# Exponent factors picked out by TensorE, the output gradient's copy moved, and more buffers, in a one-core layer kernel

## The chip, the cores and the metric

The kernel runs on one core of a Trainium2 chip. The metric is the device time of one execution in microseconds (us), of which three runs are shown. The core has TensorE (PE, with its weight loads PEld), VectorE (DVE), ScalarE (ACT), GpSimd (POOL) and SyncE (SP, which here only issues transfers). ACT and POOL issue transfers too.

## The reference

A layer with a state-space convolution and a gated feed-forward block, computed forward (`out_0`) and backward (`out_1` to `out_12`, the gradients of its inputs). L = 2048 tokens, D = 576 channels, N = 128 states per channel, F = 4608 hidden units. Cut to what matters:

```
xn = layernorm(A_u)
dt = exp(log_dt);  logdA = dt * (A_re + 1j * A_im)
K  = einsum("dn,dnl,dn->dl", C, exp(logdA * l), dt * B).real      # 576 x 2048 kernel of the convolution
s  = irfft(rfft(K) * rfft(xn)) + xn * Dskip                       # causal convolution over l
g  = silu((silu(xn @ w1) * (xn @ w3)) @ w2)
out_0 = A_u + s * g;  and the gradients for grad_out
```

`exp(logdA * l)` has a real factor exp(dt * A_re * l), which this text calls the **exponent factor**, and a sine and cosine part. With l = 64a + b each is split in a part over a (32 values) and a part over b (64 values), so per channel 96 values per state are computed.

## The kernel before, in words

**Prologue.** The tokens are loaded as 16 tiles of 128; those with an odd number are first turned back to front by a copy in DRAM (`odd_A_u`, and `odd_grad_out` for the output gradient), which later loads read. DVE makes the layer norm: statistics and scaling of the even tiles, then of the odd ones. PE turns the normalised tiles (`ln_turn`, ten sets of transposes through the PSUM pool `t_ps`, which has two buffers) and DVE copies each set to `xnT`.

**Exponent factors.** DVE multiplies dt and A_re (`rho`) and splits the product in three bf16 pieces (`pc`, in `split3`). To become the left operand of a matmul, the pieces must stand with 16 channels on the partitions: `split3` stores them in `PCS_dram[2]`, and three loads bring them back into `lhs_r` in that order. Then `early_exps` makes 54 tiles: PE multiplies `lhs_r` with the selector `sel_val` into a PSUM tile of 1024 columns (`e_ps`, two buffers), ACT takes the exponential into `E_k` (six buffers), SP stores it in `E_dram`. Many of these matmuls are issued twice, and 44 matmuls (line 370) with no use of their result run ahead of them. A Chain keeps the instructions of one engine in the order of the code; matmuls are placed behind a named lead.

**Spectra and selectors.** DVE folds the tiles (`xt<-xn_bf`), computes the angles (`thp` to `pc`, stored to `PCS_dram[0:2]`), and PE transforms the folded tokens (`early_spectrum`, line 635): 20 PSUM tiles go through `t_ps` and DVE, 12 through `e_ps` and ACT, as casts to `u_e`, stored to `UH_dram` from SP. Between them DVE builds `SEL` and the weights `Wr`, `Wi`.

**Main part.** `ffn_hidden` multiplies the tokens with w1 and w3 (lines 1121 and 1129, `pgu`), 72 steps; ACT makes `s_t` and `gu_t`, DVE `h_t`. `ssm_kernel` is woven into it: 36 chunks, each needing `lhs_t` (six small loads from `PCS_dram`), `E_l` (from `E_dram`) and matmuls into `et_ps` (line 712). Then the convolution (`ssm_conv`: `dft`, `take`, `inverse`), the feed-forward output, and the backward pass, most of the time. What stands on an engine's list is fixed by a scheduler from priorities (`pre` for the prologue, `at` later).

The copy of the odd tiles of grad_out (line 1012) is written in the convolution's `take`, but issued by GpSimd at 8.57 us.

Of the kernel before, what the change touches and what calls it, by code (L numbers as in the profile page):

```python
# [100 lines left out]
class K:  # L101
# [212 lines left out]
    def prologue(self, matp, selp, xp, gate):  # L314
# [8 lines left out]
        self.xnT = xp.tile([P, DT, L], BF16, name="xnT")  # L323
        self.PCS_dram = self.dram.tile([3, 3, D, N], BF16, name="PCS_dram")
        self.odd = {n: self.dram.tile([LT // 2, P, D], BF16, name="odd_" + n) for n in ("A_u", "grad_out", "out_0", "out_1")}
        mul = lambda e, o, a, b: e.tensor_tensor(out=o[:], in0=a[:], in1=b, op=ALU.mult)
        with pool(name="par_tmp", bufs=1) as tmp, pool(name="par_pc", bufs=2) as pcp, pool(name="sel_tmp", bufs=1) as st, \
                pool(name="ln_sb", bufs=1) as lsb, pool(name="ln_small", bufs=4) as small, pool(name="dftgen", bufs=1) as dg, \
                pool(name="ex_l", bufs=1) as lp, pool(name="ex_e", bufs=6) as ep, pool(name="ex_u", bufs=2) as up, \
                pool(name="ex_ps", bufs=2, space=PS) as eps, pool(name="t_ps", bufs=2, space=PS, side="right") as tps:  # L330
# [33 lines left out]
            self.dma_engines, self._dma_i = [self.sy, self.S], 0  # L364
            pc = self.split3(tmp, rho, 2)
            for k in range(3):
                self.sy.dma_start(out=LR_[k * 16:(k + 1) * 16], in_=self.PCS_dram[2, k].rearrange("(k p) n -> p k n", p=16))
            pw = eps.tile([P, 1024], FP32, name="e_ps")
            for k in range(44):
                nc.tensor.matmul(pw[:, 0:512], lhsT=pc[:, 2, 0, :], rhs=pc[:, 0, 0:4, :], start=True, stop=True)  # L370
            self.ln_load_odd(self.sy)
            self.pre(2)
            self.dft_phases()
            self.build_reader(SELR)
            self.pre(8)
            self.dft_sines()
# [4 lines left out]
            last = self.ln_stats(even[1:], small, last)  # L381
            self.ln_root(even, small, last)
            self.dma_engines, self._dma_i = [self.sy], 0
            turns = {14: 0, 15: 1, 20: 2, 21: 3, 22: 4, 23: 5, 24: 6, 25: 7, 26: 8, 27: 9}
            self.early_exps(SELR, LR_, ep, eps, 0, 18, turns)
            self.exps_last = self.S.prev
            next(gate)
            self.pre(18)
            self.ln_scale(even)
            self.pre(24)  # L390
            last = self.ln_stats(odd, small)
            self.ln_root(odd, small, last)
            self.ln_scale(odd)
            leads = sorted(turns)
            self.ln_turn(even, tps, leads[0:5])
            self.ln_turn(odd, tps, leads[5:10])
            self.dft_signs()
            self.dft_rows()
            self.pre(34)
            self.ln_fold()  # L400
            self.pre(38)
            thp = tmp.tile([P, DT, N], FP32, name="thp", tag="t1")
# [47 lines left out]

    def split3(self, tmp, src, q):
# [10 lines left out]
        for (c, p0, n, h, d1) in self.dsplit():  # L462
            self.dma(self.PCS_dram[q].rearrange("k (d h) n -> h d k n", h=2)[h, d1:d1 + n], pc[p0:p0 + n, :, c, :])
        return pc
# [133 lines left out]
    def early_exps(self, SELR, LR_, ep, ps, p0, p1, turns):  # L598
# [8 lines left out]
        for c2 in range(2 * p0, 2 * p1, 2):  # L607
            for o in range(0, 2 * TW, 1024):
                E = ep.tile([P, 1024], BF16, name="E_k")
                self.pre(17.5 + 1.07 * len(self.e_stores))  # L610
                pe = ps.tile([P, 1024], FP32, name="e_ps")
                n = len(self.exps)
                for k in (0, 1) if n in turns or n >= 40 else (0, 0, 1, 1):
                    ch, o1 = divmod(o + 512 * k, TW)
                    self.e_last = nc.tensor.matmul(pe[:, 512 * k:512 * k + 512], lhsT=LR_[:, c2 + ch, :],
                                                   rhs=SELR[:, o1:o1 + 512], start=True, stop=True)
                self.exps.append(self.e_last)
                self.S.activation(out=E[:], in_=pe[:], func=ACT.Exp)
                self.e_stores.append(nc.sync.dma_start(out=self.E_dram[c2 // 2, :, o:o + 1024], in_=E[:]))

    def early_spectrum(self, h, m, up, ps, name, copy, leads):
# [6 lines left out]
        for k0 in range(0, KT, 2):  # L628
            u = up.tile([P, 2, 2, 2, HW], BF16, name="u_e", tag="u" + name)
            for kt in range(k0, k0 + 2):  # L630
# [10 lines left out]
            for q in range(2):  # L641
                nc.sync.dma_start(out=self.UH_dram[2 * h + q, m, :, :, k0:k0 + 2], in_=u[:, q])

    def ssm_kernel(self, T0, TK, ps, ps1):
# [8 lines left out]
        with self.pool(name="kg_l", bufs=2) as lp, \  # L653
# [15 lines left out]
            def load_lhs(c0):  # L669
                t_ = lp.tile([P, GE, N], BF16, name="lhs_t")  # L670
                nc.gpsimd.memset(t_[:], 1.0)
                for k in range(3):
                    for q, r0 in enumerate((0, 64)):
                        nc.sync.dma_start(out=t_[r0 + k * DC:r0 + (k + 1) * DC],
                                          in_=self.PCS_dram[q, k, c0 * DC:(c0 + GE) * DC, :].rearrange("(k p) n -> p k n", p=DC))
                return t_
# [280 lines left out]
    def conv_half(self, h, T0, kp, up, rp, ypool, tp, spool, epool, ps):  # L957
# [27 lines left out]
        def take(b):  # L985
# [23 lines left out]
            self.cmul_acc(V[0], k2, kz, U[NB - 1 - b], tp, b == 0, False)  # L1009
            if h == 0 and b == NB - 1:  # L1010
                with self.tc.issue_after(self.tails[-1].ins):
                    nc.gpsimd.dma_start(out=self.odd["grad_out"][:], in_=self.turned(self.aps["grad_out"].flatten_outer_dims()))

        def inverse(m):
# [5 lines left out]
            for i in range(2):  # L1020
                even = self.idft_side(ps.tile([P, 512], FP32, name="et_ps"), V[0], 0, i, 1)
                odd = self.idft_side(ps.tile([P, 512], FP32, name="et_ps"), V[0], 1, i, 1)
                ev = epool.tile([P, W], FP32, name="ev")
                nc.scalar.copy(out=ev[:], in_=even)
                s_t = spool.tile([P, 2, W], BF16, name="s_t")
# [1060 lines left out]
def kernel(  # L2086
# [35 lines left out]
    with k.ctx:  # L2122
# [8 lines left out]
        with k.pool(name="xT", bufs=1) as xp, k.pool(name="kg_sel", bufs=1) as selp, \  # L2131
                k.pool(name="f_w", bufs=2) as wp, k.pool(name="f_gu", bufs=3) as gup, ExitStack() as fctx:
            gate = k.ffn_hidden(wp, gup)
            k.prologue(matp, selp, xp, gate)
            ktctx = ExitStack()
# [45 lines left out]
```

## Time and profile before

| | |
|---|---|
| median of three runs (lowest, highest) | 1758.78 us (1749.87, 1759.73) |
| the profiled execution | 1763.93 us, span 1762.1 us |
| PE / DVE / ACT / POOL busy | 92% / 77% / 51% / 19% |
| mean DMA rate | 234 GB/s |

The profiled execution lies 0.3% above the median; 1.8 us of it are outside the span. All starts given here are us from the span's start. In a row of the timeline stand start, duration, engine, line, operation, output and input tiles, shape and count, and in brackets how long the engine was idle before it and what ended that wait. Instructions issued through a Chain have line 86, so they are told apart by their tiles. `SPq`, `ACTq` are issues of transfers.

### The profile page before, as it was taken

The page shows a single profiled execution, that of the slowest core. Times are in us where ns is not written, and L with a number is a line of the kernel's source. Part 1 is how long each engine was busy: PE and PEld are TensorE (multiplying, and loading weights), DVE is VectorE, ACT ScalarE, POOL GpSimd, SP SyncE. Part 2 cuts the span into 40 slices and gives each one's busy share as a digit, 9 for nine tenths or more (in the row PEclk, how much of TensorE's full clock was granted, in tenths as well). Part 3 has the DMA queues.
Part 4 walks back from the last instruction along what each step waited for, and adds up shares of the span by engine and source line. Part 5 has one row for each costly group of instructions (what it writes and reads, how often), then busy time and mean ns, then how long its engine had stood idle before and what let it go on. Part 6 is the DMA issues. An engine that isn't in the chain of part 4 may idle for free. (4 is left out here: it accounts for less than half of the span.)

```text
span 1762.1 us, 34759 instructions
## 1 busy us (share of the span) xinstructions
PE 1621.4 (92%) x13740; PEld 1195.7 (68%) x13797; DVE 1361.0 (77%) x2221; ACT 893.4 (51%) x1441; POOL 329.5 (19%) x531
## 2 busy tenths in 40 slices
PE   5879998989999997989999999999998998999997
PEld 2444444454547775778888888888887776778876
DVE  7658889879784653978966989669998966877765
ACT  4878888886862112675746666654444401110001
POOL 3101111112133110111110101111111233141132
PEclk9999999999999998999999999999999999999999
DMA  7789999978799998668575767689999999999981
GB/s 205 271 259 365 349 353 341 357 252 263 245 275 254 216 203 200 178 202 227 177 198 163 200 189 211 166 252 241 234 208 252 224 256 218 228 241 222 235 174 45
DMA packets 627897, 411.92 MB, mean 234 GB/s; under 512 B 422582, under 2 KB 572342, under 8 KB 623126
## 3 DMA queue, kind: packets, MB, share of 16 engines
q1 hardware_dynamic: 580844, 283.14, 66.1%
q0 software_dynamic: 32768, 114.47, 20.4%
q10 hardware_dynamic: 14122, 12.10, 2.5%
q8 instruction: 108, 1.77, 0.4%
q14 instruction: 55, 0.45, 0.1%
HBM read 130.88 MB, written 190.89 MB: 183 GB/s over the span
## 5 line engine op out<-in xcount | busy, mean ns | idle before, releaser
L1121 PE MATMUL pgu<-wmB_w,xnT 128*128 128x512 bf16 x1101 | 269.6, 379 | 5.5 <-ACT gu_t L1134 2.4
L1965 PEld LDWEIGHTS <-acts 128*128 128x128 bf16 x2304 | 226.7, 99 | 63.7 <-DMA acts<-GU_dram 3.3
L1913 PEld LDWEIGHTS <-xn_bf 128*128 128x128 bf16 x2304 | 225.2, 98 | 37.6 <-issue 11.2
L1496 DVE TENSOR_TENSOR pr_q<-et_ps,pz 128x1024 f32<-128x1024 f32 x144 | 176.0, 1222 | 35.4 <-PE et_ps L1491 26.5
L1965 PE MATMUL px<-wT,acts 128*128 128x288 bf16 x1472 | 192.9, 289 | 0.0
L1121 PEld LDWEIGHTS <-xnT 128*128 128x128 bf16 x1152 | 106.9, 98 | 120.1 <-issue 21.3
L1499 DVE TENSOR_REDUCE S_all<-pr_q 128x32 f32<-128x1024 f32 x144 | 175.3, 1217 | 3.1
L1852 PE MATMUL ph<-w2T,goT 128*128 128x256 bf16 x1440 | 171.2, 273 | 4.5 <-ACT gh L1855 4.5
L1852 PEld LDWEIGHTS <-goT 128*128 128x128 bf16 x1440 | 139.3, 98 | 22.4 <-issue 6.4
L1894 PE MATMUL pgw<-go_o,h_n 128*128 128x288 bf16 x1152 | 148.9, 286 | 1.1 <-issue 1.1
L1134 ACT CAST gu_t<-pgu 128x1024 bf16<-128x1024 f32 x144 | 147.6, 1025 | 0.0
L1913 PE MATMUL pgw<-gu_n,xn_bf 128*128 128x256 bf16 x1152 | 134.5, 275 | 9.5 <-ACT gw L1896 9.5
L1894 PEld LDWEIGHTS <-h_n 128*128 128x128 bf16 x1152 | 111.9, 98 | 30.8 <-issue 3.3
L1913 PE MATMUL pgw<-gg_n,xn_bf 128*128 128x256 bf16 x1152 | 130.5, 273 | 0.0
L1133 ACT ACTIVATE s_t<-pgu 128x512 bf16<-128x512 f32 x144 | 88.0, 611 | 82.5 <-PE pgu L1121 44.0
L1142 POOL DMA_DIRECT2D GUF_dram<-gu_t x72 | 65.4, 908 | 338.6 <-ACT gu_t L1134 310.6
L1965 PE MATMUL px<-wA,acts 128*128 128x288 bf16 x832 | 111.6, 291 | 4.1 <-DMA acts<-GU_dram 2.7
L1916 ACT CAST gw<-pgw 128x512 bf16<-128x512 f32 x72 | 42.5, 590 | 140.0 <-PE pgw L1913 139.0
L1855 ACT CAST gh<-ph 128x512 bf16<-128x512 f32 x144 | 82.8, 607 | 59.0 <-PE ph L1852 53.7
L2032 ACT ACTIVATE go<-gx 128x576 bf16<-128x576 f32 x15 | 10.2, 683 | 187.6 <-DVE gx L2013 169.6
L1137 DVE TENSOR_TENSOR h_t<-s_t,gu_t 128x1024 bf16<-128x1024 bf16 x72 | 49.5, 688 | 50.4 <-ACT gu_t L1134 49.4
L1897 POOL DMA_DIRECT2D out_dram<-gw x36 | 20.1, 560 | 347.1 <-ACT gw L1896 274.1
(336 smaller groups left out, 3015.1 us busy)
## 6 DMA issues: line engine op xcount, KB each, us to landing
GUF_dram<-gu_t POOLq DMA_DIRECT2D x72, 512.0 KB, 5.9
H_dram<-h_t SPq DMA_DIRECT2D x72, 256.0 KB, 5.4
Q_dram<-q_k SPq DMA_DIRECT2D x36, 512.0 KB, 5.1
gg_n<-GUF_dram POOLq DMA_DIRECT2D x18, 1024.0 KB, 6.9
h_n<-GUF_dram POOLq DMA_DIRECT2D x18, 1024.0 KB, 7.8
GG_dram<-gg_n SPq DMA_DIRECT2D x36, 512.0 KB, 7.4
GU_dram<-gu_n SPq DMA_DIRECT2D x36, 512.0 KB, 4.6
E_dram<-E_k SPq DMA_DIRECT2D x54, 256.0 KB, 2.3
```

Source lines behind the costliest of these rows:

```text
L1121: ins = nc.tensor.matmul(pt, lhsT=xnT[:, c, ts], rhs=wm[w][:, c, :], start=(q == 0 and c == 0), stop=(q == 1 and c == nfull - 1))
L1133: nc.scalar.activation(out=s_t[:, :, q, :], in_=pg.rearrange("p (g f) -> p g f", g=ng), func=ACT.Silu)
L1134: nc.scalar.copy(out=gu_t[:, :, :, q, :], in_=pgu[:].rearrange("p k (g f) -> p k g f", g=ng))
L1137: self.h_last = nc.vector.tensor_tensor(out=h_t[:].rearrange("p t (g f) -> p g t f", g=ng), in0=s_t[:], in1=gu_t[:, 1], op=ALU.mult)
L1142: self.u_stores[step] = nc.gpsimd.dma_start(out=self.GUF_dram[fb * ng:(fb + 1) * ng, :, :, i0:i0 + NT, :].rearrange("g p k t f -> p k g (t ...
L1496: nc.vector.tensor_tensor(out=pr[:].rearrange("p r k e -> p r (k e)"), in0=T[x][:].rearrange("p k z d a -> p (k z d a)")[:, None].to_broad ...
L1499: nc.vector.tensor_reduce(out=self.S_all[:, :, d0:d0 + 4], in_=pr[:].rearrange("p r k (d a) -> p (r k) d a", d=4), op=ALU.add, axis=AX.X)
L1852: self.pe_last = nc.tensor.matmul(ph[j][:, k, :].rearrange("p (a f) -> p a f", f=P), lhsT=lw, rhs=rh, start=(n == 0), stop=(n == nfull))
L1855: self.sc(lambda: nc.scalar.copy(out=gh[:, j], in_=ph[j][:]))
L1894: self.pe_last = nc.tensor.matmul(pgw[pi_][:, 0:pw], lhsT=hn[:, tt, fl * P:(fl + 1) * P], rhs=go_o[:, tt, po:po + pw], start=(tt == 0), st ...
L1913: self.pe_last = nc.tensor.matmul(pw_[:, c % 2], lhsT=self.xn_bf[:, tt, c * P:(c + 1) * P], rhs=nat[:, tt, :], start=(tt == 0), stop=(tt = ...
L1965: self.pe_last = nc.tensor.matmul(px[pi_][:, 0:pw], lhsT=acts[i][:, ai, fi, :], rhs=w[:, po:po + pw], start=(n == 0), stop=(n == len(steps ...
```

## The change

1. **Exponent factors.** The pieces `pc` of `rho` are no longer stored and loaded. `row_picks` makes 0/1 matrices, and `pick_rows` multiplies them with the pieces: 6 matmuls of 32 x 128 per column of `lhs_r`, 216 in all, in five groups, through `t_ps`; DVE casts the result into `lhs_r` (six casts, 96 partitions, 256 to 1024 columns). The matmuls on `lhs_r` now use 96 partitions. The 44 matmuls of line 370 go, and the first 24 tiles' matmuls are no longer issued twice.
2. **Order.** The sines of the Fourier matrix come ahead of everything on ACT. The exponents are written in five portions between the parts of the layer norm, the transposes and the fold.
3. **Buffers.** Every second `E_k` uses a buffer of the feed-forward's pools (`s_t`, `h_t`), so that there are twelve. The pool of `u_e` for DVE has four buffers rather than two, and ACT's `u_e` uses the three of `gu_t`.
4. **GpSimd stores.** ACT's 12 `u_e` casts are stored by GpSimd (12 transfers), and it also loads the first `lhs_t` (6).
5. **grad_out's copy** is issued by ACT, behind the last `ev` copy of the convolution's first half.

```diff
-            nc.vector.memset(LR_[:], 0.0)
+            self.row_picks(tmp)
 ...
-            last = self.ln_stats(even[0:1], small)
+            self.dft_phases()
+            self.dft_sines()
 ...
-            pc = self.split3(tmp, rho, 2)
-            for k in range(3):
-                self.sy.dma_start(out=LR_[k * 16:(k + 1) * 16], in_=self.PCS_dram[2, k].rearrange("(k p) n -> p k n", p=16))
-            pw = eps.tile([P, 1024], FP32, name="e_ps")
-            for k in range(44):
-                nc.tensor.matmul(pw[:, 0:512], lhsT=pc[:, 2, 0, :], rhs=pc[:, 0, 0:4, :], start=True, stop=True)
+            pc = self.split3(tmp, rho, 2, store=False)
             self.ln_load_odd(self.sy)
 ...
+            self.pick_rows(pc, LR_, tps, 0, (2, 6))
+            exps(0, 4)
 ...                                          # loads of the rates, ln_stats(even)
+            self.pick_rows(pc, LR_, tps, 8, (8,), 2)
+            exps(4, 8)
 ...                                          # ln_root, ln_scale(even), ln_stats(odd)
+            self.pick_rows(pc, LR_, tps, 16, (8,), 14)
+            exps(8, 12)
 ...                                          # ln_root, ln_scale(odd), both ln_turn
+            self.pick_rows(pc, LR_, tps, 24, (8,), 28)
+            exps(12, 16)
 ...                                          # dft_signs, dft_rows, ln_fold
+            self.pick_rows(pc, LR_, tps, 32, (4,), 38)
+            exps(16, 18)
 
+    def row_picks(self, pool):
+        self.picks = pool.tile([P, 2, 20, 32], BF16, name="picks", tag="Wr")
+        nc.vector.memset(self.picks[:], 0.0)
+        for h in range(2):
+            nc.vector.tensor_copy(out=self.picks[:, h, 0:16, h:16:2], in_=self.ident_bf[:].rearrange("p (o e) -> p o e", e=8))
+
+    def pick_rows(self, pc, rows, ps, c0, counts, lead=None):
+        pt = ps.tile([P, 2 * 512], FP32, name="t_ps")
+        lead = self.exps[lead].ins if lead else None
+        for k in range(3):
+            for j in range(sum(counts)):
+                for h in range(2):
+                    b, o = divmod(h * cfg.D // 2 + 8 * (c0 + j), P)
+                    with self.tc.issue_after(lead) if lead else nullcontext():
+                        nc.tensor.matmul(pt[32 * k:32 * k + 32, j * N:(j + 1) * N], lhsT=self.picks[:, h, o // 8, :],
+                                         rhs=pc[:, k, b, :], start=(h == 0), stop=(h == 1))
+        j = 0
+        for m in counts:
+            self.V.tensor_copy(out=rows[0:96, c0 + j:c0 + j + m, :],
+                               in_=pt[0:96, j * N:(j + m) * N].rearrange("p (c n) -> p c n", n=N))
+            j += m
 ...
-                E = ep.tile([P, 1024], BF16, name="E_k")
+                E = (self.gup.tile([P, 1024], BF16, name="E_k", tag="sh"[n // 2 % 2] + "_t") if n % 2 else
+                     ep.tile([P, 1024], BF16, name="E_k"))
-                for k in (0, 1) if n in turns or n >= 40 else (0, 0, 1, 1):
+                for k in (0, 1) if n in turns or n >= 40 or n < 24 else (0, 0, 1, 1):
 ...
-            u = up.tile([P, 2, 2, 2, HW], BF16, name="u_e", tag="u" + name)
+            u = (self.gup if name == "e_ps" else up).tile([P, 2, 2, 2, HW], BF16, name="u_e", tag="gu_t" if name == "e_ps" else "ue")
-                nc.sync.dma_start(out=self.UH_dram[2 * h + q, m, :, :, k0:k0 + 2], in_=u[:, q])
+                (nc.gpsimd if name == "e_ps" else nc.sync).dma_start(out=self.UH_dram[2 * h + q, m, :, :, k0:k0 + 2], in_=u[:, q])
 ...
-                        nc.sync.dma_start(out=t_[r0 + k * DC:r0 + (k + 1) * DC], ...
+                        (nc.sync if c0 else nc.gpsimd).dma_start(out=t_[r0 + k * DC:r0 + (k + 1) * DC], ...
 ...                                          # in take(b): no longer
-                with self.tc.issue_after(self.tails[-1].ins):
-                    nc.gpsimd.dma_start(out=self.odd["grad_out"][:], in_=self.turned(self.aps["grad_out"].flatten_outer_dims()))
 ...                                          # in inverse(m), cp = the ev copy
+            if h == 0 and m == 0:
+                self.at(T0 + self.CONV_INVERSES[0][0] + 8)
+                with self.tc.issue_after(cp.ins):
+                    nc.scalar.dma_start(out=self.odd["grad_out"][:], in_=self.turned(self.aps["grad_out"].flatten_outer_dims()))
```

ACT's list at the program's start, before and then after (`dft_fr` are the angles, `cCS` the sines and cosines):

```order
L86 ACTIVATE dft_fr<-irow,dft_t 128x512 x2
L86 DMA PCS_dram<-pc 128x3x128
L86 DMA PCS_dram<-pc 96x3x128
L86 DMA PCS_dram<-pc 64x3x128
L86 ACT_TABLE_LOAD
L86 ACTIVATE cCS<-dft_fr 128x1024
L86 ACTIVATE dft_q<-dft_fr 128x1024
```

```order
L86 ACTIVATE dft_fr<-irow,dft_t 128x512 x2
L86 ACT_TABLE_LOAD
L86 ACTIVATE cCS<-dft_fr 128x1024
L86 ACTIVATE dft_q<-dft_fr 128x1024
L86 ACTIVATE cCS<-dft_q,halfpi_col 128x1024
L86 ACT_TABLE_LOAD
L86 ACTIVATE E_k<-e_ps 128x1024 x54
```

The three stores of the pieces are gone, and the sines follow the angles directly.

DVE's list between the layer norm's fold and the angles, before and then after; `xt` are the folded tokens, `thp` the first of the angles, `lhs_r` the exponents' left operand (the numbers tell the four token tiles apart):

```order
L86 TENSOR_TENSOR xt_156<-xn_bf 128x1152 x2
L86 TENSOR_TENSOR xt_157<-xn_bf 128x1152 x2
L86 SCALAR_TENSOR_TENSOR thp<-A_im_bf,dt_col 128x640
L86 TENSOR_SCALAR sr_t<-thp 128x640
L86 TENSOR_TENSOR thr<-thp,sr_t 128x640
```

```order
L86 TENSOR_TENSOR xt_156<-xn_bf 128x1152 x2
L86 TENSOR_TENSOR xt_157<-xn_bf 128x1152 x2
L86 CAST lhs_r<-t_ps 96x512
L86 SCALAR_TENSOR_TENSOR thp<-A_im_bf,dt_col 128x640
L86 TENSOR_SCALAR sr_t<-thp 128x640
L86 TENSOR_TENSOR thr<-thp,sr_t 128x640
```

The last of the six casts into `lhs_r` stands between the two, and it needs PE's last picks, which stand behind the matmuls of exponent tile 38. The other five stand ahead of the fold.

POOL's list around the first `lhs_t`, before and then after:

```order
L124 DMA PCS_dram<-pc 128x3x128 x2
L124 DMA PCS_dram<-pc 32x3x128
L124 DMA PCS_dram<-pc 128x3x128
L671 MEMSET lhs_t 128x768 x2
L1142 DMA GUF_dram<-gu_t 256x2x512 x7
```

```order
L124 DMA PCS_dram<-pc 128x3x128
L672 DMA UH_dram<-u_e 256x1x288 x8
L701 MEMSET lhs_t 128x768 x2
L704 DMA lhs_t<-PCS_dram 16x6x128 x2
L672 DMA UH_dram<-u_e 256x1x288 x2
L704 DMA lhs_t<-PCS_dram 16x6x128
L672 DMA UH_dram<-u_e 256x1x288 x2
L704 DMA lhs_t<-PCS_dram 16x6x128 x3
L1174 DMA GUF_dram<-gu_t 256x2x512 x7
```

The last three loads of the first `lhs_t` now stand behind the stores of ACT's last `u_e`. On PE the first matmuls that read `lhs_t` stand behind 23 matmuls of the wide kind of the feed-forward, where 48 stood ahead of them before.

More of the change, by code (lines that the diff above doesn't have):

```diff
@@ L323, in prologue @@
         self.xnT = xp.tile([P, DT, L], BF16, name="xnT")
-        self.PCS_dram = self.dram.tile([3, 3, D, N], BF16, name="PCS_dram")
+        self.PCS_dram = self.dram.tile([2, 3, D, N], BF16, name="PCS_dram")
         self.odd = {n: self.dram.tile([LT // 2, P, D], BF16, name="odd_" + n) for n in ("A_u", "grad_out", "out_0", "out_1")}
@@ L380, in prologue @@
             self.load_rates(tmp)
-            last = self.ln_stats(even[1:], small, last)
-            self.ln_root(even, small, last)
[L383 to L388, printed above, removed]
+            last = self.ln_stats(even, small)
+            self.pre(12)
+            self.pick_rows(pc, LR_, tps, 8, (8,), 2)
+            self.dma_engines, self._dma_i = [self.sy], 0
+            exps(4, 8)
+            self.pre(15)
+            self.ln_root(even, small, last)
             self.ln_scale(even)
-            self.pre(24)
+            self.pre(20)
             last = self.ln_stats(odd, small)
+            self.pick_rows(pc, LR_, tps, 16, (8,), 14)
+            exps(8, 12)
+            self.pre(26)
             self.ln_root(odd, small, last)
             self.ln_scale(odd)
-            leads = sorted(turns)
             self.ln_turn(even, tps, leads[0:5])
             self.ln_turn(odd, tps, leads[5:10])
+            self.pick_rows(pc, LR_, tps, 24, (8,), 28)
+            exps(12, 16)
+            self.pre(30)
             self.dft_signs()
@@ L400, in prologue @@
             self.ln_fold()
+            self.pick_rows(pc, LR_, tps, 32, (4,), 38)
+            exps(16, 18)
+            self.exps_last = self.S.prev
+            next(gate)
             self.pre(38)
@@ L461, in split3 @@
                 r = r2
-        for (c, p0, n, h, d1) in self.dsplit():
+        for (c, p0, n, h, d1) in self.dsplit() if store else ():
             self.dma(self.PCS_dram[q].rearrange("k (d h) n -> h d k n", h=2)[h, d1:d1 + n], pc[p0:p0 + n, :, c, :])
```

32 lines of the change are left out of this document (17 added, 15 removed).

## The prediction

> **What bounds the kernel now.** First the page's engine shares, then the windows by stage, then PE's waits from the first feed-forward matmul to the convolution's end.
>
> ```profile
> PE 1621.4 (92%) x13740; PEld 1195.7 (68%) x13797; DVE 1361.0 (77%) x2221; ACT 893.4 (51%) x1441; POOL 329.5 (19%) x531
> 100.00:110.00 10.00, 6.14 (x43) 4.22 (x43) 8.19 (x12) 8.05 (x15) 0.00 (x0) 1.00 0.82 245
> 180.00:230.00 50.00, 48.34 (x364) 24.22 (x370) 44.94 (x89) 42.45 (x76) 8.92 (x10) 1.00 1.00 360
> PE et_ps L866 <- ACT kraw L869: 5.6, 7, 2.0
> ```
>
> Between 180 and 230 us PE is busy 48.3 of 50, and its costliest wait comes to 5.6 us in 450. What starts PE's steady stretch earlier therefore shortens the program by about as much. Before it lies the prologue, where PE works 6 of 10 us and waits for others. Its path is read from the timeline:
>
> ```profile
> 29.72 2.32 PE L615 MATMUL e_ps<-sel_val,lhs_r 128*128 128x512 bf16 x5 [6.88 <-DMA lhs_r<-PCS_dram]
> 31.65 1.02 ACT L86 ACTIVATE E_k<-e_ps 128x1024 bf16<-128x1024 f32 x1 [12.29 <-PE e_ps L615]
> 62.58 5.43 DVE L86 TENSOR_TENSOR xt<-xn_bf 128x1152 bf16<-128x1152 bf16 x8
> 67.93 0.82 DVE L86 SCALAR_TENSOR_TENSOR thp<-A_im_bf,dt_col 128x640 f32<-128x640 bf16 x1
> 78.32 1.42 DVE L86 CAST u_e<-t_ps 128x576 bf16<-128x576 f32 x2
> 94.17 1.94 ACT L86 ACTIVATE E_k<-e_ps 128x1024 bf16<-128x1024 f32 x2 [0.59 <-DMA E_dram<-E_k]
> 94.90 0.14 DVE L86 TENSOR_SCALAR rq<-pcol 128x1 f32<-128x1 f32 x1
> 104.55 0.82 DVE L86 TENSOR_TENSOR Wi<-Wi,dt_col 128x640 f32<-128x640 f32 x1
> 112.66 1.46 PE L1121 MATMUL pgu<-wmB_w,xnT 128*128 128x512 bf16 x6
> ```
>
> The exponents run from 31.65 to 96.1 us. Behind them DVE sets the pace: angles from 67.93, the first twelve `u_e` casts from 78.32 to 94.9, selectors and weights to 105.4, and 7.3 us later PE is in its steady stretch. Two groups tell what those stretches lose:
>
> ```profile
> L86 ACT ACTIVATE E_k<-e_ps 128x1024 bf16<-128x1024 f32 x54 | 52.2, 1026 | 24.5 <-PE e_ps L615 16.3 <-DMA E_dram<-E_k 7.5 <-PE t_ps L635 0.5
> L86 DVE CAST u_e<-t_ps 128x576 bf16<-128x576 f32 x18 | 12.9, 753 | 10.2 <-DMA UH_dram<-u_e 7.0 <-PE t_ps L635 3.1
> ```
>
> The twelve casts need 12 x 0.753 = 9.0 us and take 16.6; 7.0 us of the waits are for stores of the two `u_e` buffers.
>
> **The change, part by part. Start of the exponents.** The sines and the pieces take these rows:
>
> ```profile
> 3.82 1.33 ACT L86 ACTIVATE dft_fr<-irow,dft_t 128x512 f32<-128x512 f32 x2 [0.30 <-DVE dft_t L86]
> 6.45 0.81 DVE L86 TENSOR_TENSOR rho<-A_re_bf,dt_col 128x640 f32<-128x640 bf16 x1
> 10.56 0.69 DVE L86 TENSOR_SCALAR dft_q<-dft_fr 128x1024 f32<-128x1024 f32 x1
> 12.42 1.81 DVE L86 SCALAR_TENSOR_TENSOR sel_val<-sel_dl,pm,sel_val 128x1536 bf16<-128x1536 bf16 x1
> 14.87 1.06 ACT L86 ACTIVATE cCS<-dft_fr 128x1024 bf16<-128x1024 f32 x1
> 18.07 1.28 ACT L86 ACT_TABLE_LOAD   x1
> 11.53 0.15 PEld L370 LDWEIGHTS <-pc 128*128 128x128 bf16 x1 [0.28 <-issue]
> 15.77 6.57 PEld L370 LDWEIGHTS <-pc 128*128 128x128 bf16 x31 [0.25 <-issue]
> 52.96 0.61 PE L250 MATMUL t_ps<-ident_bf,xn_bf 128*128 128x128 bf16 x8
> 53.88 0.61 PE L250 MATMUL t_ps<-ident_bf,xn_bf 128*128 128x128 bf16 x8
> 55.56 1.22 DVE L86 CAST xnT<-t_ps 128x1024 bf16<-128x1024 f32 x1 [0.35 <-PE t_ps L256]
> ```
>
> The angles end at 5.2 us; DVE's two phase operations (10.56 to 12.42) then end near 7.2; the sines (14.87 to 18.07) and the table behind them take 4.5, so ACT is free near 11.8. DVE's `rho` and pieces (6.45 to 10.6, 4.2 us) now end near 11.5 and `sel_val` at 13.3. One pick is 128 columns wide. The 512-wide matmuls of line 370 came every 0.43 us at first (a load of 0.15 behind a pause of 0.28), so a pick at that clock is 0.107 us, and the first 48, behind the first piece at 8.7, end near 13.9; eight later 128-wide matmuls took 0.61 us, 0.076 each. A cast of 1024 columns is 1.22 us, of 256 some 0.35. First exponent on ACT: **15.5 us, 16 earlier**.
>
> **What becomes of the 16 us.** The cadence of the exponents:
>
> ```profile
> 41.80 1.99 ACT L86 ACTIVATE E_k<-e_ps 128x1024 bf16<-128x1024 f32 x2 [0.20 <-PE e_ps L615]
> 51.45 8.46 ACT L86 ACTIVATE E_k<-e_ps 128x1024 bf16<-128x1024 f32 x9 [0.24 <-PE e_ps L615]
> ```
>
> A tile costs 1.09 us where its matmuls are doubled (1.99 and a wait of 0.20 for two) and 0.94 where not (8.46 for nine). Tiles 0 to 27 are now single (26.3 us), 28 to 38 double (12.0). PE's list puts the picks and transposes into long blocks, and ACT has only two PSUM tiles to live on: the 41 picks behind tile 3 (3.1 us, 2 lost), 48 behind tile 14 (3.6, 2.6 lost), the last eight sets of transposes with only two exponent tiles among them (7.3 us by the 0.92 from set to set at 52.96 and 53.88, 4.5 lost), 48 picks (3.6 lost): 12.7 us. The matmuls of tile 38 end near 15.5 + 26.3 + 12.0 + 12.7 - 1 = 65.5. Only then may PE do the last 24 picks (1.8), DVE the cast (0.64) and `thp`: **near 68, as before (67.93)**. DVE is no sooner done: its last copies to `xnT` end near 54 by the same count, the fifth picks and their cast near 57, then come the 5.43 us fold and small work, so it is free near 64 and waits some 3 us for the picks. The 16 us are used up by three things: ACT's starvation, the fifth portion's place behind the fold, and DVE's casts.
>
> **Where time comes from.** Of the 16.6 us of the twelve casts, the store waits should go: four buffers instead of two, the exponents nearly done when the casts begin (fifteen tiles of 0.94 behind tile 38 and the last picks, near 83 rather than 96), and ACT's stores off SP's list. Least possible is 9.0; with half of the group's waits for PE, cut to twelve of eighteen casts, I take 10.1, which moves weights and steady PE **6.5 us earlier**, to 106.2. Bounds: `thp` 2 us earlier or 4 later (a pick between 0.053 us, a quarter of 0.21, and 0.08), the casts at 9.0 or 13: between 2 and 10 us.
>
> **What is late next: `lhs_t`.** Its loads move from SP to POOL, behind the last `u_e` stores, and PE asks for it after 23 wide matmuls rather than 48. Rows:
>
> ```profile
> L1012 POOL DMA_DIRECT2D odd_grad_out<-in_grad_out_dram x1: 1339/1339/1339, 8.6 to 8.6; - x1
> L1028 POOL DMA_DIRECT2D S_dram<-s_t x16: 706/717/730, 410.9 to 531.3; - x16
> S_dram<-s_t POOLq DMA_DIRECT2D x16, 144.0 KB, 4.9
> UH_dram<-u_e SPq DMA_DIRECT2D x32, 144.0 KB, 2.3
> L1556 POOL DMA_DIRECT2D X_b<-in_A_B_re_dram x10: 501/527/530, 1397.9 to 1695.1; - x10
> 110.78 0.64 ACT L86 CAST u_e<-e_ps 128x576 bf16<-128x576 f32 x1 [0.16 <-PE e_ps L635]
> 118.15 0.61 PE L1129 MATMUL pgu<-wtail,xnT 64*128 64x512 bf16 x4
> ```
>
> In the old times: last cast ends at 111.4; two stores of the same 256 pieces (0.72 each), three loads (0.53), then landing, which no row shows for such a load on POOL; nearest are 2.3 us on SP and 4.9 on POOL. I take 4.9: 119.4 to 119.9. PE has done its 23 at 117.9 (24 by the row at 118.15). PE waits **2.0 us**, 0 to 4, and everything in its list with it. The other UH stores on POOL cost nothing while the casts of `Wr` and `Wi` (10 us of DVE) lie above them; if that cover went, a store 2.6 us later would hold up ACT's fourth to sixth `u_e`.
>
> **grad_out's copy on ACT.** In the convolution ACT stops for the issue, with `s_t` of the next step queued behind it. No row shows 1024 pieces on this queue:
>
> ```profile
> L1956 ACTq DMA_DIRECT2D go<-odd_grad_out x8: 326/327/928, 1427.7 to 1572.3; - x8
> L181 SPq DMA_DIRECT2D out_dram<-odd_out x8: 725/4291/6005, 815.4 to 1109.8; - x8
> 23.10 2.26 SPq L86 DMA_DIRECT2D xt<-odd_A_u  x4
> L1208 POOL DMA_DIRECT2D go_t<-odd_grad_out x8: 537/537/557, 518.6 to 663.7; - x8
> ```
>
> Between 0.33 and 6.0 us; four loads of 256 pieces took 2.26, the same number of pieces, and I take that. ACT waits for PE half a microsecond per feed-forward step, so PE loses **1 us**, 0 to 5. Its first reader is at 518.6, over 50 us later, so landing is hidden. Its leaving the start is worth nothing beyond the above.
>
> At nothing: twelve `E_k` buffers (their 7.5 us of waits lie within the stretch now paced by PE and DVE); 36 doubled matmuls fewer (PE waits there); the chunk order (after nine chunks both lists stand at 192 wide matmuls).
>
> Sum: -6.5 + 2.0 + 1.0 = **-3.5 us**: 1760.4 for the profiled execution (1763.93, its span and 1.8 around it), 1755 by the median (1758.78), which lies 0.3% lower.
>
> **Rivals.** *DVE takes it back*: the casts stay at 13 us, or `thp` comes 4 us late; the steady stretch starts 2 to 3 us earlier, the two new waits eat it, 1758 to 1759. For it speaks that DVE gets 5.5 us more work; against, that its waits of 10.2 us leave room. *The new waits stay away*: `lhs_t` lands in 2.3, the issue costs 0.3, and the casts run at 9.0: 1749.
>
> *Slower: PE stays at half clock.* The window shows the clock dropping over a wait:
>
> ```profile
> 20.00:30.00 10.00, 3.12 (x15) 1.21 (x13) 5.54 (x24) 0.00 (x0) 2.09 (x3) 0.80 0.99 132
> ```
>
> Line 370's matmuls ran at 0.43 us for 5.1 us and then at 0.21 (31 in 6.57); they go, as does doubling in the first 24 tiles. From 15.5 to tile 38 PE has 100 exponent matmuls (0.43 cold), 144 picks (0.107) and ten sets (1.3): 71 us cold, to 87 instead of 65.5, so 21.5 later: about 1777. Cold work costs half its time, so it undoes the gain from 7 us of it on. Against: the first picks are a busy stretch of 5 us themselves, and nine single tiles kept 0.94 us each. The Trainium skill ("TensorE: Matmul & The Clock Gate", Part 1, the table of the two states) has half rate as the default, full rate after about 3.4 us of sustained work, and half again after an idle window of that length. By that rule, the blocks and gaps below 3.4 us here would leave the sum as it is; the trace's 5.1 us is slower than its figure.
>
> *GpSimd is held up by DVE*: were the five issues behind the last cast to take the 1.34 us of the longest POOL issue rather than 0.72 and 0.53, `lhs_t` would be 3.7 us later: 1759. The Trainium skill ("SBUF — State Buffer", SBUF: two separate sides, the warning on DMAs from GpSimd) says that such an issue stalls while VectorE runs a two-port operation. The trace does not show it: 706 to 730 ns, the whole spread, at a busy DVE.
>
> **How the numbers follow.** Chances: forecast 0.50, DVE takes it back 0.22, the new waits stay away 0.14, GpSimd held up 0.07, half clock 0.07. Low end: 10 gained, and medians that scatter by 5 (the three runs lie 9.9 apart): 1744. High end: 2 gained, 4 and 5 lost, and half that scatter: 1768. Only the half clock lies beyond. 1% is 17.6 us, about what this kernel's measurement can tell from no change; faster needs more than any sum here gives, which leaves 0.04 for what I overlook; slower has the half clock and 0.01.
>
> **What would show it.** First `E_k` near 15.5 us; last near 83; `thp` near 68 behind a wait of DVE for the last picks; twelve casts in about 10 us; steady PE near 106; PE waiting some 2 us at `et_ps` for `lhs_t`; ACT's copy near 2.3 us. Wrong, if `thp` starts before 64 or after 72, or if a later stage takes up the shift.

## The result: 11 us faster, most of it where the prediction did not look

The changed kernel takes 1743.9 us (median of 22 runs, 1735.02 to 1768.29), the kernel before, beside it, 1758.4 (22 runs, 1740.24 to 1779.36). The ratio is **0.9937, 95% interval 0.9914 to 0.9961**: 11 us faster, 7 to 15. The ratio leaves out runs over 1.5% above the fastest of their kernel; with them the medians lie 14.5 us apart. The forecast was 1755 (-3.5 us), and the median lies at the low end of its range (1744). The profiled execution took 1749.26 us, its span is 1747.5 (before: 1762.1).

First the page's engine shares, then the timeline of the start, in the profile of the change:

```profile
PE 1626.2 (93%) x13933; PEld 1202.8 (69%) x13933; DVE 1369.9 (78%) x2229; ACT 892.3 (51%) x1441; POOL 342.2 (20%) x548
3.64 3.92 DVE L86 CAST pmf<-pmt 128x2 f32<-128x2 int32 x1
17.30 3.77 ACT L86 ACTIVATE E_k<-e_ps 128x1024 bf16<-128x1024 f32 x4 [1.27 <-PE e_ps L645]
68.88 0.69 DVE L86 CAST lhs_r<-t_ps 96x512 bf16<-96x512 f32 x1 [2.98 <-PE t_ps L472]
69.49 0.81 DVE L86 SCALAR_TENSOR_TENSOR thp<-A_im_bf,dt_col 128x640 f32<-128x640 bf16 x1
79.88 1.41 DVE L86 CAST u_e<-t_ps 128x576 bf16<-128x576 f32 x2
91.11 0.14 DVE L86 TENSOR_SCALAR rq<-pcol 128x1 f32<-128x1 f32 x1
100.91 0.82 DVE L86 TENSOR_TENSOR Wi<-Wi,dt_col 128x640 f32<-128x640 f32 x1
110.25 1.46 PE L1153 MATMUL pgu<-wmB_w,xnT 128*128 128x512 bf16 x6
118.43 0.82 PE L743 MATMUL et_ps<-SEL,lhs_t 128*128 128x256 bf16 x6 [2.84 <-DMA lhs_t<-PCS_dram]
```

The exponents start 14 us earlier (17.30, before 31.65), `thp` 1.6 later, the twelve casts end 3.8 earlier (91.11, before 94.90), and steady feed-forward work begins 2.4 earlier (110.25, before 112.66). PE waits 2.84 us for `lhs_t`.

To see how the lead grows, the same instructions of PE are looked up in both timelines: behind the convolution's longest wait, 8 us later, around the moved copy, at the first output matmul (`po`), at the last group of the output stretch, and at the first matmul of the backward pass (`ph`). Before:

```profile
369.19 0.65 PE L866 MATMUL et_ps<-KT,dS 128*128 128x288 bf16 x4 [1.99 <-ACT kraw L869]
377.55 0.60 PE L1129 MATMUL pgu<-wtail,xnT 64*128 64x512 bf16 x4
463.27 0.65 PE L866 MATMUL et_ps<-KT,dC 128*128 128x288 bf16 x4 [1.01 <-ACT kraw L869]
531.99 2.26 PE L1217 MATMUL po<-w2a,hcA 128*128 128x288 bf16 x17
679.20 6.79 PE L1217 MATMUL po<-w2a,hcC 128*128 128x288 bf16 x32 [9.49 <-DMA hcC<-H_dram]
691.23 2.46 PE L1852 MATMUL ph<-w2T,goT 128*128 128x256 bf16 x21
```

After:

```profile
367.25 0.65 PE L897 MATMUL et_ps<-KT,dS 128*128 128x288 bf16 x4 [1.99 <-ACT kraw L900]
369.13 1.17 PE L897 MATMUL et_ps<-KT,dC 128*128 128x288 bf16 x4
377.29 0.60 PE L1161 MATMUL pgu<-wtail,xnT 64*128 64x512 bf16 x4
462.99 0.66 PE L897 MATMUL et_ps<-KT,dC 128*128 128x288 bf16 x4 [1.64 <-DVE s_t L1055]
531.73 2.50 PE L1249 MATMUL po<-w2a,hcA 128*128 128x288 bf16 x19
669.52 4.09 PE L1249 MATMUL po<-w2a,hcC 128*128 128x288 bf16 x32 [1.01 <-DMA hcC<-H_dram]
678.86 2.46 PE L1884 MATMUL ph<-w2T,goT 128*128 128x256 bf16 x21
```

The lead is 1.94 us, then 0.26, 0.28 and 0.26; at the last output group it is 9.7, at the backward pass 12.4, and at the end 14.6. So of this pair's 14.6 us, 0.3 come from all that the prediction weighed, 12.1 from the **output stretch** (from the first `po` to the first `ph`, 159.2 us before and 147.1 after), and 2.2 from the 1070 us behind it. The wait at `hcC` is 8.5 us of the 12.1. It costs another 2.7 behind it: the same 32 matmuls take 6.79 us before and 4.09 after, and from 674 to 685 us the granted clock before was 0.53 (after, from 669 to 680, it was 1.00).

What is different there shows in SP's rows and in the landing times between 560 and 665 us. Before, then after:

```profile
616.66 10.64 SPq L1775 DMA_TRANSPOSE hcB<-H_dram  x1
628.59 6.32 SPq L1775 DMA_TRANSPOSE hcC<-H_dram  x1
636.17 8.83 SPq L1775 DMA_TRANSPOSE hcA<-H_dram  x1
...
665.84 8.54 SPq L1775 DMA_TRANSPOSE hcC<-H_dram  x1
x_t<-odd_A_u POOLq DMA_DIRECT2D x5, 144.0 KB, 7.3
```

```profile
612.60 4.66 SPq L1807 DMA_TRANSPOSE hcB<-H_dram  x1
621.92 4.97 SPq L1807 DMA_TRANSPOSE hcC<-H_dram  x1
631.24 4.61 SPq L1807 DMA_TRANSPOSE hcA<-H_dram  x1
x_t<-odd_A_u POOLq DMA_DIRECT2D x5, 144.0 KB, 3.7
```

Each step of the stretch takes a load of `hcA`, `hcB` or `hcC` (1.18 MB, turned on its way). The duration in such a row is how long issuing the load held SP; the data land after that. After the change, from 575 to 645 us, six of eight loads take 4.4 to 5.0 us (two take 6.1 and 6.2), and each starts 9.3 us behind the one before, one PE step. Before, each takes 6 to 11 us, SP has no pause between them, GpSimd's loads of `x_t` from `odd_A_u` land in 7.3 us rather than 3.7, and the list runs ever later. PE does not feel it until the end: there four `w2T` loads and four of `w2r` stand ahead of the last `hcC`, which is issued at 665.84 us, and PE waits 9.5 us. (The change has the same order, but issues that load at 655.48 us.) Call the two patterns **late** and **on time**.

### The profile page after: what moved, and what is told of

It is laid out like the page before. It is cut to its first block, busy times and chain, and to the rows that moved or that the text cites. A ratio compares the mean times of both kernels' runs of the same rounds, so it can differ in the third digit from the quotient of the medians.

```text
span 1747.5 us, 35087 instructions
## 1 busy us (share of the span) xinstructions
PE 1626.2 (93%) x13933; PEld 1202.8 (69%) x13933; DVE 1369.9 (78%) x2229; ACT 892.3 (51%) x1441; POOL 342.2 (20%) x548
## 5 line engine op out<-in xcount | busy, mean ns | idle before, releaser
L1153 PE MATMUL pgu<-wmB_w,xnT 128*128 128x512 bf16 x1152 | 276.9, 380 | 2.5 <-ACT gu_t L1166 2.4
L1945 PEld LDWEIGHTS <-xn_bf 128*128 128x128 bf16 x2304 | 224.8, 98 | 36.4 <-issue 10.2
L1948 ACT CAST gw<-pgw 128x512 bf16<-128x512 f32 x72 | 42.5, 591 | 141.9 <-PE pgw L1945 140.9
```

What stands on the lines that cost most here:

```text
L1153: ins = nc.tensor.matmul(pt, lhsT=xnT[:, c, ts], rhs=wm[w][:, c, :], start=(q == 0 and c == 0), stop=(q == 1 and c == nfull - 1))
L1945: self.pe_last = nc.tensor.matmul(pw_[:, c % 2], lhsT=self.xn_bf[:, tt, c * P:(c + 1) * P], rhs=nat[:, tt, :], start=(tt == 0), stop=(tt = ...
```

## The experiments

All runs in one table: the ratio to the kernel before, then from the profile the first `E_k`, the first `po`, the median duration of eight loads from 42 us behind it, PE's wait at `hcC`, and the length of the stretch (us). The profiles are of one execution each; two of the same instructions (the change and planes3) differ by 2.7 us at the first `po`.

| kernel | ratio (95%) | first E_k | first po | load | hcC | stretch |
|---|---|---|---|---|---|---|
| before | | 31.6 | 532.0 | 8.0 | 9.5 | 159.2 |
| before_again | 0.9998 (0.9966, 1.0029) | 30.3 | 534.6 | 8.5 | 7.8 | 155.2 |
| copy_pool | 1.0007 (0.9977, 1.0037) | 31.0 | 538.8 | 7.5 | 6.1 | 153.9 |
| hcc_first | 0.9977 (0.9947, 1.0007) | 31.4 | 537.8 | 6.8 | 0 | 149.9 |
| copy_only | 0.9949 (0.9917, 0.9982) | 26.1 | 530.9 | 4.6 | 0 | 145.2 |
| copy_ue | 0.9987 (0.9951, 1.0022) | 25.6 | 526.6 | 6.4 | 6.6 | 155.7 |
| ue_hcc | 0.9953 (0.9919, 0.9987) | 25.9 | 531.0 | 4.7 | 0 | 145.2 |
| the change | 0.9937 (0.9914, 0.9961) | 17.3 | 531.7 | 4.6 | 1.0 | 147.1 |
| planes3 | 0.9946 (0.9914, 0.9977) | 17.2 | 529.0 | 4.8 | 0 | 145.2 |
| copy_back | 0.9977 (0.9944, 1.0010) | 17.3 | 539.5 | 4.5 | 0 | 145.2 |
| lhs_sp | 0.9958 (0.9925, 0.9990) | 17.0 | 534.4 | 4.6 | 0 | 145.2 |
| warm | 0.9944 (0.9910, 0.9977) | 17.4 | 527.2 | 4.6 | 0 | 145.8 |
| junk | 1.0009 (0.9975, 1.0042) | 17.3 | 532.0 | 7.2 | 9.5 | 160.1 |
| warm_hcc | 0.9935 (0.9905, 0.9965) | 17.4 | 529.9 | 4.6 | 0 | 150.6 |

**before_again**: no edit.

> The kernel before, once more. In the first pair of profiles the changed kernel is only 1.9 us ahead at 200 us and 0.3 ahead at 500; 11.5 of its gain arises between 620 and 684 us, where the kernel before waits 9.5 us for the load of hcC. Theory A (the wait belongs to the program): the wait of 8 to 10 us at hcC is there again, and the time is 1758, ratio 1.00. Theory B (the wait is an accident of one execution): the wait at hcC is under 3 us in this profile, the ratio of the timed runs is still 1.00, and the median of the changed kernel gains its 14 us elsewhere.

The wait is there again, in the view of PE's waits from 560 to 720 us:

```profile
PE po L1217 <- DMA hcC<-H_dram: 7.8, 1, 7.8
```

So it is no accident of one execution: theory A.

**copy_only**: the kernel before with one edit.

```diff
-            if h == 0 and b == NB - 1:
-                with self.tc.issue_after(self.tails[-1].ins):
-                    nc.gpsimd.dma_start(out=self.odd["grad_out"][:], ...
+            if h == 0 and m == 0:
+                self.at(T0 + self.CONV_INVERSES[0][0] + 8)
+                with self.tc.issue_after(cp.ins):
+                    nc.scalar.dma_start(out=self.odd["grad_out"][:], ...
```

> The kernel before with nothing changed but grad_out's copy: on ACT's queue in the convolution instead of on GpSimd's at the start. Theory A1 (the copy sets the output stretch right): the wait at hcC falls from 9.5 to 1 us and the time by some 10 us, to 1748. Theory A2 (it is the prologue's change, or the shifted addresses): the wait stays at 9.5 and the time rises by the 0.7 us of the issue, 1759. Theory B: the wait comes or not by chance; the time stays within 3 us of 1758.

The copy's move alone brings 9 us (3 to 15), where the whole change brings 11. PE's list and SP's are the same as before. Part of it is gained at the start: the stored pieces of `rho` come back sooner. In SP's rows, before and then with the copy moved:

```profile
10.67 2.30 SPq L86 DMA_DIRECT2D PCS_dram<-pc  x3
21.66 1.40 SPq L86 DMA_DIRECT2D lhs_r<-PCS_dram  x3
```

```profile
12.86 1.38 SPq L86 DMA_DIRECT2D PCS_dram<-pc  x3
16.56 1.40 SPq L86 DMA_DIRECT2D lhs_r<-PCS_dram  x3
26.15 1.94 ACT L86 ACTIVATE E_k<-e_ps 128x1024 bf16<-128x1024 f32 x2 [5.60 <-PE e_ps L615]
```

From the first store to the loads it took 11.0 us with the copy beside it (9.6 or 9.7 in the three other profiles of that start) and 3.7 without (4.7 and 4.9 in copy_ue and ue_hcc). The rest is the stretch, on time in this profile. By itself this looked like theory A1.

**copy_back**: the change with the old place of the copy (the edit above, reversed).

> The changed kernel with grad_out's copy back on GpSimd at the start. The profile of the change shows 0.78 us for the issue and 1.6 us of PE's wait for s_t behind it. If the copy costs that and nothing else: 0.7 to 1 us faster than the change, 1743. Theory A1 (the copy's place brings the gain of the output stretch): the wait at hcC is back at some 9 us and the time near 1754. Theory A2: the wait stays near 1 us.

The stretch is on time with the copy at the start, so the copy's place alone does not set it: **A1 falls**, as far as one profile can tell. The 7.8 us are lost earlier. The copy's place changes the scheduler's list, so that 32 matmuls for ACT's spectra now stand ahead of DVE's (the row has the first 24); ten of the twelve casts wait for them:

```profile
83.59 5.67 PE L665 MATMUL e_ps<-xt,cCS 128*128 128x288 bf16 x24
91.17 7.42 DVE L86 CAST u_e<-t_ps 128x576 bf16<-128x576 f32 x10 [9.86 <-PE t_ps L665]
```

**planes3**: the change with one number back, so that all DRAM tiles behind it keep their old addresses.

```diff
-        self.PCS_dram = self.dram.tile([2, 3, D, N], BF16, name="PCS_dram")
+        self.PCS_dram = self.dram.tile([3, 3, D, N], BF16, name="PCS_dram")
```

> The changed kernel with PCS_dram at its old size of three planes, so that every later DRAM tile lies where it lay before; every instruction is the same. If the addresses in DRAM set the output stretch: the wait at hcC is back at some 9 us and the time near 1754. If not: as the change, 1744, wait near 1 us.

The time is the change's and the stretch is on time: addresses are not it.

**copy_pool**: copy_only with `nc.gpsimd` in place of `nc.scalar`.

> The kernel before with grad_out's copy still on GpSimd's queue, but issued in the convolution. With the copy on ACT there, the first exponent came 5.5 us earlier, PE's hundredth feed-forward matmul 4.7 us earlier, and the wait at hcC (9.5 and 7.8 us in two profiles of the kernel before) was gone. Theory P (what costs is the copy's traffic at the start): the same here, hundredth matmul near 136, wait under 2, ratio 0.995. Theory Q (1024 pieces on GpSimd's queue disturb its later loads): the start gains the same 4.7, but the wait at hcC is again near 8, and the time is near 1755.

The edit did not do what it was meant to: on GpSimd's list the copy stayed at the start.

```profile
L1031 POOL DMA_DIRECT2D odd_grad_out<-in_grad_out_dram x1: 1119/1119/1119, 8.5 to 8.5; - x1
PE po L1218 <- DMA hcC<-H_dram: 6.1, 2, 5.3
```

It serves as another run of the kernel before (1.0007, stretch late). Queue and place are not told apart.

**copy_ue**: copy_only with four `u_e` buffers, ACT's `u_e` in `gu_t`'s buffers, and its stores on GpSimd.

```diff
-... pool(name="ex_u", bufs=2) as up, ...
+... pool(name="ex_u", bufs=4) as up, ...
-            u = up.tile(..., tag="u" + name)
+            u = (self.gup if name == "e_ps" else up).tile(..., tag="gu_t" if name == "e_ps" else "ue")
-                nc.sync.dma_start(out=self.UH_dram[...
+                (nc.gpsimd if name == "e_ps" else nc.sync).dma_start(out=self.UH_dram[...
```

> The kernel before with the copy on ACT, and beside it four u_e buffers for DVE, ACT's u_e in the hidden layer's buffers and its stores on GpSimd. Theory 1 (the prediction's: the stores of two buffers held up the casts): the twelve casts take 11 us instead of 16.6, steady PE is 5 us earlier than with the copy alone, and the time falls to 1740. Theory 2 (another engine is next): the casts then wait for PE, which works off the exponents until 89 us; 14 us or more, and 2 us gained at most.

Theory 2: the casts run from 71.7 to 88.6 us, with the copy alone from 72.2 to 88.8. The buffers do not shorten them while the exponents run beside them until 92 us. What the start gains, the stretch gives back: it is late, though the copy is on ACT.

**lhs_sp**: the change with the first `lhs_t` loads on SP.

```diff
-                        (nc.sync if c0 else nc.gpsimd).dma_start(
+                        nc.sync.dma_start(
```

> The changed kernel with the first lhs_t loads back on SP. PE waits 2.8 us for them in the profile of the change (1.8 in that of the same program with three planes). If GpSimd's queue makes them late: the wait goes, and steady PE gains 2 us, 1742. If the wait is of PE's asking early, behind 23 wide matmuls: SP has its own stores ahead of the loads, the wait is as long or longer, and the time as the change or 2 us more.

The wait goes, but the list has PE ask at 122.2 us rather than 118.4, and the first `po` is no earlier (534.4, the change 531.7). The interval cannot tell 2 us.

**warm**: the change with the first 24 tiles doubled.

```diff
-                for k in (0, 1) if n in turns or n >= 40 or n < 24 else (0, 0, 1, 1):
+                for k in (0, 1) if n in turns or n >= 40 else (0, 0, 1, 1):
```

> The changed kernel with the first 24 exponent tiles' matmuls doubled as before. The granted clock was 0.53 between 40 and 50 us in the profile of the change, and fifteen tiles that should take 0.94 us took 1.0 to 1.1. Theory H (half clock slows the start): with more for PE the clock stays above 0.9 there and thp comes 2 us earlier or more. Theory S (PE is not what the tiles wait for): 24 tiles of 1.09 rather than 0.94 us cost 3.6 us on ACT, thp comes as late as before or 2 later, and the time is within 3 us of 1744.

The windows from 40 to 50 us, the change and then this kernel (the granted clock is the third number from the end), and this kernel's `thp`:

```profile
40.00:50.00 10.00, 8.87 (x36) 3.96 (x34) 5.37 (x16) 7.37 (x9) 0.00 (x0) 0.53 0.93 323
40.00:50.00 10.00, 8.73 (x82) 5.02 (x80) 8.64 (x19) 8.82 (x10) 0.00 (x0) 1.00 0.83 280
66.72 0.81 DVE L86 SCALAR_TENSOR_TENSOR thp<-A_im_bf,dt_col 128x640 f32<-128x640 bf16 x1
```

PE does 82 matmuls instead of 36 in the same 10 us, `thp` comes 2.8 us earlier and the first `po` 4.5: theory H. Of the 4.5, part may be chance: warm_hcc, below, has the same instructions up to there, `thp` again at 66.7, and its first `po` is 1.8 earlier. In the timed runs (0.9944) nothing shows.

**hcc_first**: the kernel before with one index.

```diff
-            with self.tc.issue_after(self.hc_loads[13].ins) if gi == 0 else nullcontext():
+            with self.tc.issue_after(self.hc_loads[14].ins) if gi == 0 else nullcontext():
```

> The kernel before with one edit on SP's list: the last hcC load of the output stretch stands ahead of the four w2T and four w2r loads instead of behind them; every other list is word for word the same. In three profiles of the kernel before and its like, the loads of the stretch ran back to back, 6 to 12 us each, and PE waited 5 to 10 us at this one. Theory L (SP's list is late there, and what stands ahead of the load makes the wait): the wait at hcC falls under 2 us, the loads before it stay at 6 to 12 us, and the time falls by 7 to 9 us, ratio 0.995. Theory M (the loads are slow, whatever stands ahead): the next load, of hcA, or w2T is then as late, the wait moves there, and the time stays within 3 us of before.

Theory L holds for the wait: the loads stay at 5 to 11 us, the wait at `hcC` is gone, and a smaller one is left (PE's waits, 560 to 720 us):

```profile
PE po L1217 <- DMA hcA<-H_dram: 2.6, 2, 1.6
```

The stretch is 149.9 us, 4 to 9 shorter than in the three late profiles of the kernel before. The gain in time, 4 us, is less than expected and not certain: its interval runs from 9 gained to 1 lost.

**ue_hcc**: copy_ue with that index.

> grad_out's copy on ACT in the convolution, the u_e buffers and GpSimd stores, and the load of hcC ahead of w2T. Without the last edit the start was 5.9 us earlier than in the kernel before, but the wait at hcC was 6.6 us and the time 0.999. Theory L: the wait goes, 6 and 7 us add up: 0.992, faster than the changed kernel. Theory M: 0.998.

The stretch ran on time in the profile, so the index had nothing to do there. The same instructions up to 650 us were late in copy_ue: **what decides is not in the program alone.**

**junk**: the change with a useless transfer at the start of the stretch. PE, DVE, GpSimd and SP have the same lists; ACT's has the one transfer more.

```diff
             finish(second)
+            junk = self.dram.tile([P, LT // 2 * D], BF16, name="junk")
+            with self.tc.issue_after(self.sgos[-1].ins):
+                nc.scalar.dma_start(out=junk[:], in_=self.aps["grad_out"].flatten_outer_dims()[0:LT // 2 * P].rearrange("(p a) d -> p (a d)", p=P))
```

> The changed kernel with a useless copy of 1.18 MB between two DRAM tiles on ACT's queue just as the output stretch begins; all lists are otherwise the same, and nothing reads the copy. Theory S (the stretch has two ways to run: a delay at its entry makes SP late, its loads then overlap GpSimd's and stay slow): the loads take 6 to 11 us for the whole 100 us that follow, far longer than the copy itself lasts, the wait at hcC is back at 5 to 10 us, and the time is 1752. Theory T (a load is slow only while something else uses the queues): the loads near the copy are slow, two or three steps later they take 4.6 us again, and the time is as the change.

The transfer lasts 3.1 us: all its 1.18 MB lie in the window from 559 to 563 (first row, by queue), between 559.1 and 562.2. The other rows are SP's loads from there on, and PE's wait:

```profile
q10 hardware_dynamic: 48, 1.18, 69.1%
558.40 9.96 SPq L1810 DMA_TRANSPOSE hcB<-H_dram  x1
569.65 12.44 SPq L1810 DMA_TRANSPOSE hcC<-H_dram  x1
610.87 10.85 SPq L1810 DMA_TRANSPOSE hcA<-H_dram  x1
640.54 7.35 SPq L1810 DMA_TRANSPOSE hcA<-H_dram  x1
PE po L1249 <- DMA hcC<-H_dram: 9.5, 3, 7.3
```

All that theory S foretold came, also in the timed runs. Three microseconds of traffic at the entry make the loads slow for 95 us, bring the wait back in full and cost all that the change had gained (1.0009). Up to there PE's timeline is the change's own to within 1 us, and from the first `po` to 0.3.

**warm_hcc**: warm with the index of hcc_first.

> The changed kernel with the first 24 exponent tiles doubled again and the last hcC load ahead of w2T. With the doubling alone steady PE was 3.5 us earlier than in the change by the three-hundredth feed-forward matmul and the time 0.9944; the order of the loads makes a difference only in executions whose output stretch runs late. If both hold: 0.991 to 0.993, some 2 to 4 us faster than the change. If the start's gain is lost further on, as 1.9 us were in the convolution of the change, 0.994.

The best ratio of the table, and not told apart from the change. Its entry was slow too, but here PE itself waited early, and the following loads came on time:

```profile
548.62 9.90 SPq L1807 DMA_TRANSPOSE hcA<-H_dram  x1
578.07 4.95 SPq L1807 DMA_TRANSPOSE hcA<-H_dram  x1
PE ptr L1310 <- DVE go_o L1267: 3.6, 1, 3.6
```

**What the table says together.** Every profile has a load of `hcC` that starts 32 to 40 us behind the first `po`. Where it ended within 40.3 us of that `po`, the stretch was on time from there (seven profiles); where it ended at 42.0 or later, late (six), but for warm_hcc (42.5), which paid 3.6 us and had its slack back. All four profiles with the old list up to there are late; all six with the change's exponents, junk apart, are on time from there; of the three with the old exponents and the copy on ACT, one is late. This tells the two patterns apart, and early; it is not yet a cause. When PE arrives does not decide: a first `po` at 526.6 us (copy_ue) was followed by a late stretch, one at 539.5 (copy_back) by one on time. The loads of a stretch on time leave SP a few microseconds of slack per step. That a late load overlaps GpSimd's loads of the next step, and so stays slow, fits the rows and was not isolated; what in the change makes the entry quicker **stays open**: not the copy's place, not addresses, not `lhs_t`'s queue, each by one profile. How often the timed runs of a kernel are late, no run shows.

## Why the prediction was right in direction and short by two thirds

1. *First `E_k` at 15.5*: 17.30. The term that failed is DVE's way to the phases, put at an end near 7.2 us: the `pmf` cast took 3.92 us (0.44 before), and the phases ended at 10.2.
2. *`thp` near 68, behind a 3 us wait for the last picks*: 69.49, behind 2.98 us. That 14 us gained would be used up was right. The last `E_k` ended at 87.2 rather than near 83.
3. *Twelve casts in 10.1 us*: 11.2. *Steady PE 6.5 earlier*: 2.4. Of the missing 4.1 us, `thp`'s 1.6 and the casts' 1.1 are two thirds; the remainder lies between the weights and PE (9.3 us, before 8.1). copy_ue adds that the buffers give this only with the exponents out of the way.
4. *PE waits 2.0 us for `lhs_t`*: 2.84, as the last load landed 6.1 us behind its issue rather than 4.9. That GpSimd is held up by DVE did not come: its last five issues start 0.52 to 0.58 us apart, not 1.34. *The copy's issue costs 1.0*: ACT is held 0.78 us, PE waits 1.64 instead of 1.01 at 463 us, so 0.6.
5. *The copy's "leaving the start is worth nothing beyond the above"*: false. With the old list, taking the copy away from the stores is worth 4 to 5.5 us of the first exponent (26.1, against 30.3 to 31.6); in the change its return costs 7.8 us by the first `po`, through the scheduler's list.
6. *Half clock* had 0.07 as a rival at 1777. It came in part: the granted clock was 0.53 from 40 to 50 us. Without that `thp` is 2.8 us earlier and the first `po` 1.8 to 4.5 (warm_hcc, warm), so the 36 doubled matmuls that the prediction put "at nothing" were worth something in these profiles. In the convolution it took another 1.7 in this pair: behind the same wait of 1.99 us, the change's groups of four matmuls came every 0.9 us for 3.6 us (the row at 369.13), before every 0.49. That is not the change's doing: in before_again the granted clock fell there too (0.66 from 370 to 375 us). The Trainium skill ("TensorE: Matmul & The Clock Gate", Part 1, table of the two states) has half rate return after an idle window of about 3.4 us. The trace shows it behind a wait of 1.99, and behind the same wait not in the profile of before; how long half rate lasted (3.6) agrees with the page's 3.4 for getting back.
7. *The sum, -3.5*: its terms, as measured in this pair, are -2.4, +2.8 and +0.6, so +1.0, and the pair's lead at the first `po` is 0.3. The four profiles with the old list reach the first `po` at 535.8 us on average, the three with the change's list at 530.9: -4.9, where the four spread over 7. That this is near -3.5 does not confirm the terms, and that the measured time came out at the low end of the range, and not below it, is luck: most of the gain came from a stretch that the sum does not contain. (The rival at 1749 does not follow from its own terms either: casts of 9.0 instead of 16.6 us save 7.6, which gives 1751.)
8. **The step that failed** is the choice of views. The prediction read PE's waits from the first feed-forward matmul to the convolution's end, near 560 us. The longest single wait of PE in the whole program lies 110 us behind that. The page's groups do not list it, but PE's waits from 560 to 720 us have it first:

```profile
PE po L1217 <- DMA hcC<-H_dram: 9.5, 1, 9.5
```

   Neither its price nor the SP list ahead of it was weighed. The three late profiles of the kernel before have a stretch of 156.1 us on average, the change 147.1: -9, against -3.5 for all that was forecast.

## What to carry to other kernels

Read the waits of the bounding engine to the very end before pricing an edit at the start: a long wait far behind it may depend on how the program arrives there. Where one queue issues the loads of every step, a short burst of other traffic can leave them late for long (here 3 us of it for 95 us); so give the stretch's last load its place ahead of loads that are needed later, and look whether the queue has pauses. Compare several profiles of each kernel before a difference of 10 us in one stretch is put down to an edit, and try the suspected disturbance on the good kernel, not only the repair on the bad one.

## What was not expected of the hardware

- **A 3 us burst with a memory of 95 us** (junk): loads of 1.18 MB that held SP 4.6 us each (256 GB/s) went to a median of 7.2, and SP had no pause in which to catch up.
- **A cast of two numbers took 3.92 us.** In all seven profiles with the change's exponents it is the same 3.92, in the seven others 0.44 or 0.45. GpSimd makes its iotas just then, 3.11 to 8.11 us. The cast before, then two rows of GpSimd in the profile of the change:

```profile
3.94 0.44 DVE L86 CAST pmf<-pmt 128x2 f32<-128x2 int32 x1
4.34 1.20 POOL L530 IOTA sel_val<- 128x512 bf16 x2
6.08 2.03 POOL L530 IOTA sel_val<- 128x512 bf16 x3
```

  The cast begins 0.3 us earlier than before (3.64, not 3.94) and ends at 7.56, just behind one of these iotas (7.53), before at 4.38, just behind the first (4.35). The Trainium skill ("SBUF — State Buffer", SBUF: two separate sides) describes a port pair of VectorE and GpSimd that one instruction holds to its end while the other is blocked. The ends agree with it. Whether this cast is one that needs the pair, and why five iotas went past it, no run here shows; the cause stays open.
